# Loading V of three batches densely and spreading it on GpSimd: sparse attention before a squared-ReLU MLP, one core

## The chip, the cores and the metric

The kernel runs on one core of one Trainium2 chip. The metric is the device time of one execution in microseconds; the time given for a kernel is the median of several runs. Below, PE is TensorE, DVE is VectorE, ACT is ScalarE, POOL is GpSimd, and SP is the SyncE, whose queue issues DMAs here.

## The reference

Attention in 8 batches of 8 heads over 576 positions of 64 elements. The first four heads of a batch use a local causal mask (32 wide), the last four a strided one (same position modulo 32). The result becomes a matrix x of 4608 tokens by 512 and goes through an MLP with a squared ReLU.

```python
scores = scale * np.matmul(q, k.transpose(0, 1, 3, 2))
rel = pos[:, None] - pos[None, :]
mask_local = (rel >= 0) & (rel < 32)
mask_strided = (rel >= 0) & (pos[None, :] % 32 == pos[:, None] % 32)
attn = softmax(np.where(mask, scores, -1e9))
x = (attn @ v).transpose(0, 2, 1, 3).reshape(B * S, H * D)
h = np.maximum(x @ w_in, 0.0)
out = (h * h) @ w_out
```

## The kernel before

A unit is one batch and one pair of heads; units 4b and 4b+1 of batch b are local, 4b+2 and 4b+3 strided. A strided unit is gathered so that 8 blocks of 72 rows stand densely, and only those blocks are computed. Each unit has steps: T (transposes of q and k on PE, local units of the early batches), S (scores, matmul at L346 into four PSUM banks, exponentials on ACT at L325, masks on DVE at L360), D (the product with V at L487, in two parts for a local and three for a strided unit, each followed by a reciprocal and a scaling on DVE at L499 and L500, which also free the PSUM bank), and E (the transposition of the result into `xt`). V tiles have a further column of ones, so that a row takes VP = 72 places of which 64 come from memory; the product gives the softmax sum as well.

The MLP runs in 9 chunks of 512 tokens: mm1 (L547, 16 groups of four matmuls, ReLU on ACT at L553, square on DVE at L556) and mm2 (L587, 16 groups). The order is written out by hand: a list of MLP groups, a list of attention steps, and `due`, which says how many attention steps stand ahead of each group. Batches 0 and 1 have an order of their own; batches 2 to 7 are a stream that starts at group 32. `hooks` holds further work to be issued ahead of a given group, put there by `at`, `second` and `plan`. Every engine runs its own instructions in the order in which they were issued, so a waiting instruction holds up what stands behind it on its engine. The MLP and attention share PE in that order.

Loads. DMAs issued from POOL convert f32 to bf16 on the way. For batches 2 to 4 these are:

- `load_qk_local_sw` (L132): rows of q and k of the local units, cast (copied into another layout) later by `cast_qk_local` (L142) on DVE and ACT;
- `cast_str_dram` (L167): q and k of the strided units into a DRAM tile `q_d`, `k_d`, which `transpose_str` (L175) brings in transposed, by a DMA transpose on the SP queue, as `qT_s` and `kT_s`;
- `load_v_local_sw` (L239, L240): V of the local units straight into `vl_all`, in runs of 64 elements;
- `load_v_str_direct` (L689): V of the strided units straight into the tiles `vss` (`vs` in the profile), also in runs of 64 elements, four DMAs per batch.

`load_v_local_gated` puts a one-element copy on POOL ahead of V (L677) that reads the last transposed tile of the batch: so POOL waits for the DMA transposes of that batch, and all that it issues later comes after them. `hold_sync(4)` (L681) is a tiny DMA on SP that reads V of batch 4: so SP's DMA transposes of batch 4 wait for the landing of that V. V and the DMA waits are released through slots: `vls` and `vss` have four tiles each, used by two batches in turn (batches 2 and 4 use the same two).

From batch 5 on, `loads_qk` and `loads_v` load q, k and V as f32 from the SP queue, and POOL casts them (L142, L222, L223, L254). The cast of strided V, `cast_v_str` at L254, is the function that the change uses for batches 2 to 4 as well. `load_v_str_sw(b)` stands in the file before and after; before the change nothing calls it. It loads strided V of one batch in one DMA into a staging tile `v_st` (72 partitions, rows of 512 elements, bf16); a load of the same shape at L439 serves batches 0 and 1.

The vl_st memsets of two staging tiles (L875) stand at hook 50.

Of the kernel before, what the change touches and what calls it, by code (L numbers as in the profile page):

```python
# [9 lines left out]
BF16 = mybir.dt.bfloat16  # L10
# [4 lines left out]
def kernel(  # L15
# [9 lines left out]
    nc = tc.nc  # L25
    B, H, S, D = q.shape
# [7 lines left out]
    NJ = 8  # L34
    RH = STRIDE // NJ
    SP_ = RH * NA
    NBS = 2 * NJ
    VP = 72

    singles = ctx.enter_context(tc.tile_pool(name="singles", bufs=1))  # L40
# [12 lines left out]
    dram = ctx.enter_context(tc.tile_pool(name="dram", bufs=2, space=bass.MemoryType.DRAM))  # L53
# [16 lines left out]
    NV = 4  # L70
# [4 lines left out]
    vl_all = singles.tile([128, NV, 2, NL, VP], BF16, name="vl")  # L75
    vls = [vl_all[:, i] for i in range(NV)]
    vss = [singles.tile([SP_, NBS, VP], BF16, name=f"vs{i}") for i in range(NV)]
    vl_sts = [singles.tile([128, 2 * NL, D], FP32, name=f"vl_st{i}") for i in range(2)]
# [4 lines left out]
    w_in_b = singles.tile([128, 4, d_ff], BF16)  # L83
    w_out_b = singles.tile([128, 16, d_model], BF16)

    ones = singles.tile([128, D], BF16)
    bias_l = w_out_b[:, 12:14, :].rearrange("p a c -> p (a c)")[:, 0:S].rearrange("p (a t c) -> p a t c", a=2, c=QL)
    bias_s = w_out_b[0:SP_, 14, 0:S // 2].rearrange("p (t c) -> p t c", c=SP_)
# [9 lines left out]
    units = [(b, p) for b in range(B) for p in range(H // 2)]  # L98
    st = {}
# [4 lines left out]
    LB = 5  # L104
    PAIRS = 22

    def load_qk_local(u, eng, gate=None):
        b, p = units[u]
        s = st.setdefault(u, {})
        for name, src in (("q", q), ("k", k)):  # L110
            t = qk_st.tile([QL, 2, 6 * D], FP32, name=f"{name}_st")
            if gate is not None and name == "q":
                nc.gpsimd.tensor_copy(t[0:1, 0, 0:1], gate)
            if b >= LB:
                for hh in range(2):
                    eng.dma_start(out=t[:, hh].rearrange("p (t d) -> p t d", d=D),
                                  in_=src[b, 2 * p + hh].rearrange("(t p) d -> p t d", p=QL))
                s[name + "f"] = t
                continue
            eng.dma_start(out=t, in_=src[b, 2 * p:2 * p + 2]  # L120
                          .rearrange("h (p j) d -> p h (j d)", j=6))
            s[name + "f"] = t
# [13 lines left out]
    def cast_qk_local(u, copies, names="qk"):  # L136
        s = st[u]
        for name, copy in zip("qk", copies):
            if name not in names:
                continue  # L140
            t = qk_in.tile([QL, 6, 2, D], BF16, name=f"{name}_l")
            copy(t.rearrange("p j h d -> p h j d"),  # L142
                 s[name + "f"].rearrange("p h (j d) -> p h j d", j=6))
            s[name] = t
# [17 lines left out]
    came = {}  # L162

    def cast_str_dram(b):
        for name, src in (("q", q), ("k", k)):
            t = dram.tile([4 * SP_, NJ * D], BF16, name=f"{name}_d")
            nc.gpsimd.dma_start(  # L167
                out=t.rearrange("(x y) c -> x (y c)", x=16),
                in_=src[b, H // 2:H].rearrange("h (x y) d -> (h x) (y d)", x=4))
            big[b, name] = t  # L170

    def transpose_str(b):
        for name in "qk":
            o = strT.tile([128, NJ // 2, 4 * SP_], BF16, name=f"{name}T_s")
            nc.sync.dma_start_transpose(out=o, in_=big.pop((b, name)))  # L175
            came[b] = o[0:1, 0, 0:1]
            for i in range(2):
                st.setdefault(4 * b + 2 + i, {})[name + "T"] = o[:, :, 2 * SP_ * i:2 * SP_ * (i + 1)]
# [16 lines left out]
    def transpose_local(u):  # L195
        s = st[u]
        for name in "qk":
            if name == "k":
                full = kTl[v_slot(u)]
                dst = full[:, 32:32 + S]  # L200
            else:
                full = dst = qkT.tile([128, S], BF16, name="qk"[u % 2] + "T")
            nc.sync.dma_start_transpose(out=dst.rearrange("c (t p) -> c t p", p=QL),
                                        in_=s[name].rearrange("p t h d -> p (t h d)"))
            s[name + "T"] = full

    def v_slot(u):
        b, p = units[u]
        return (b * 2 + p % 2) % NV
# [18 lines left out]
    def load_v_str_sw(b):  # L228
        t = v_st.tile([SP_, 2, NJ * D], FP32, name="v_st")
        t = t.rearrange("p h c -> p (h c)").bitcast(BF16).rearrange("p (h c) -> p h c", h=4)  # L230
        nc.gpsimd.dma_start(out=t, in_=v[b, 4:8].rearrange("h (p j) d -> p h (j d)", j=NJ))
        for i in range(2):
            st.setdefault(4 * b + 2 + i, {})["vf"] = t[:, 2 * i:2 * i + 2]

    def load_v_local_sw(b, u0=0, nu=2):
        i = (2 * b + u0) % NV
        t = vl_all[:, i:i + nu].rearrange("p u h t d -> p (u h t) d")[:, :, 0:D]
        src = v[b, 2 * u0:2 * (u0 + nu)].rearrange("h (t p) d -> p (h t) d", p=QL)
        nc.gpsimd.dma_start(out=t[32:128], in_=src)  # L239
        nc.gpsimd.dma_start(out=t[0:32, 1:2 * nu * NL], in_=src[64:96, 0:2 * nu * NL - 1])  # L240
        for u in range(nu):
            st.setdefault(4 * b + u0 + u, {})["v"] = vls[i + u]
# [8 lines left out]
    def cast_v_str(u, copy=None):  # L251
        s = st[u]
        t = vss[v_slot(u)]
        (copy or nc.gpsimd.tensor_copy)(t[:, :, 0:D], s["vf"].rearrange("p h (j d) -> p (h j) d", d=D))  # L254
        s["v"] = t
# [417 lines left out]
        load_v_str_first(1)  # L673
        load_w_out(3)

    def load_v_local_gated(b):
        nc.gpsimd.tensor_copy(vl_all[64:65, (2 * b) % NV, 0, 0, 0:1], came[b])  # L677
        load_v_local_sw(b)

    def hold_sync(b):  # L680
        nc.sync.dma_start(out=dram.tile([1, 2], BF16, name="hold"),  # L681
                          in_=vss[v_slot(4 * b + 3)][0:1, NBS - 1, 0:2])

    def load_v_str_direct(b):
        for u in (4 * b + 2, 4 * b + 3):
            t = vss[v_slot(u)]
            h = 2 * units[u][1]
            for i in range(2):
                nc.gpsimd.dma_start(out=t[:, NJ * i:NJ * (i + 1), 0:D],  # L689
                                    in_=v[b, h + i].rearrange("(p j) d -> p j d", j=NJ))  # L690
            st.setdefault(u, {})["v"] = t

    def loads_qk(b):
        for i in range(2):
            load_qk_local(4 * b + i, nc.sync)
        cast_str_dram(b)
        for i in range(2):
            cast_qk_local(4 * b + i, pool2)

    def loads_v(b):  # L700
        for i in range(2):
            load_v_local(4 * b + i, nc.sync)
        for i in range(2):
            load_v_str(4 * b + 2 + i, nc.sync)
        for i in range(2):
            cast_v_local(4 * b + i)
        for i in range(2):
            cast_v_str(4 * b + 2 + i)
# [109 lines left out]
    def at(n, fn):  # L818
        hooks.setdefault(n, []).append(fn)

    def plan(b, g0, g1, n0=None):
        if b < LB:
            at(g0, lambda: transpose_str(b))
            for i in range(2):
                copies = dve2 if b == 2 else (nc.scalar.copy, nc.vector.tensor_copy)
                at(g1 + 2 * i, lambda u=4 * b + i, c=copies: cast_qk_local(u, c))
            return
        g = g0 + (g1 - g0) * 45 // 100
        tr, tl = max(g + 8, g0 + (g1 - g0) * 8 // 10), (g + 14, g + 18)
        at(g, lambda: loads_qk(b))  # L830
        at(tr, lambda: transpose_str(b))
        at(n0, lambda: loads_v(b))
        for i in range(2):
            at(tl[i], lambda u=4 * b + i: transpose_local(u))

    def second(n, *fns):
        for fn in fns:
            at(n, fn)
# [25 lines left out]
    rows = lambda b: (lambda: load_qk_local_sw(b, (4 * b, 4 * b + 1)))  # L864
    second(14, rows(2), lambda: cast_str_dram(2))
    plan(2, 28, 28)
    second(29, lambda: load_v_local_gated(2), lambda: load_v_str_direct(2), rows(3), lambda: cast_str_dram(3))
    done_prev, g_prev = 0, 32
    plan(3, 42, 46)
    second(43, lambda: load_v_local_gated(3), rows(4), lambda: load_v_str_direct(3), lambda: cast_str_dram(4))  # L870
    second(60, lambda: load_v_local_sw(4), lambda: load_v_str_direct(4))
    second(64, lambda: hold_sync(4))
    plan(4, 64, 61)
    for t in vl_sts:
        second(50, lambda t=t: nc.gpsimd.memset(t[0:32], 0.0))  # L875
    for b in range(2, B):
        g_end, s_end = ready.get(b, starts[b]), ends[4 * b + 3]
        total = sum(weights[g_prev:g_end])
# [49 lines left out]
```

## Time and profile before

| | us |
|---|---|
| median of 5 runs (307.31 to 308.35) | 307.95 |
| the profiled execution, whole | 307.48 |
| its span | 305.8 |
| PE busy in the span | 296.6 |
| DVE busy | 158.1 |
| ACT busy | 166.1 |
| POOL busy | 75.4 |

Busy times are shares of the whole span; the stages differ. From 56 to 125 us, where the loads of batches 2 to 5 are issued and used, DVE and ACT are busier than on average: between 66 and 70 us DVE is busy for 3.77 of 4 us and ACT for 3.70, while PE has 3.95. Start times in the timelines below are in us from the start of the span, and the number after the engine's line is the source line. Matmuls overlap in the pipeline, so the time of a group is read from its start to the start of the next one. The chain of waits follows the work that ended last back from the end; a DMA piece in it runs from issue to landing, and other work may have gone on beside it.

### The profile page before, as it was taken

The numbers are of one execution on the slowest core, as the hardware profiler recorded it, in microseconds if no ns is written. First come the engines' busy times: TensorE is split into PE (matmuls) and PEld (weight loads), VectorE is DVE, ScalarE is ACT, GpSimd is POOL, SyncE is SP. The second block draws the span as 40 slices with busy tenths as digits, with TensorE's granted clock in tenths as the row PEclk, the third lists the DMA queues.
The fourth block names the chain that finished last, engine by engine and source line by source line (L and its number), as shares of the span: only waits on it lengthen the run. The fifth ranks groups of instructions, "written<-read, shape, count | busy, mean of one in ns | idle before, by whom it ended". The sixth has DMA issues, their size and how long they took to land.

```text
span 305.8 us, 6066 instructions
## 1 busy us (share of the span) xinstructions
PE 296.6 (97%) x2328; PEld 150.0 (49%) x2368; DVE 158.1 (52%) x406; ACT 166.1 (54%) x335; POOL 75.4 (25%) x105
## 2 busy tenths in 40 slices
PE   8989999999999999999999999999999999999995
PEld 3644464555555544445445545544444444444444
DVE  4558646578777776665748586364422222222200
ACT  4748748787667765545545456453344443444311
POOL 8753300540882033630272060000000000000000
PEclk9999999999999999999999999999999999999999
DMA  8999997996999999999899682122220001000121
GB/s 154 162 204 205 190 208 144 222 167 144 139 200 158 165 201 217 212 191 183 194 253 213 152 194 65 49 71 67 86 68 35 34 35 36 34 34 36 62 76 70
DMA packets 94118, 40.75 MB, mean 133 GB/s; under 512 B 78858, under 2 KB 87754, under 8 KB 93898
## 3 DMA queue, kind: packets, MB, share of 16 engines
q0 software_dynamic: 34528, 15.00, 39.3%
q1 hardware_dynamic: 59562, 25.37, 36.5%
q8 instruction: 18, 0.29, 0.4%
q14 instruction: 10, 0.08, 0.1%
HBM read 37.63 MB, written 13.57 MB: 167 GB/s over the span
## 4 chain that ended last, share of the span: by engine, by line
PE 82%; DMA 6%; issue 6%; POOL 4%; DVE 1%; ACT 0%; POOLq 0%; DVEq 0%
PE ph L547 35%; PE py L587 28%; PE ph L587 4%; PE pt L587 3%; DMA vs<-in_v_dram 3%; PE pt L487 3%; DMA w_out_b<-in_q_dram 2%; PE pt L346 2%; PE pt L547 1%; DMA kT_s<-k_d 1%; PE pt L569 1%; POOL vs L689 1%; PE pt L523 1%; PE pt L410 1%; POOL q_st L132 1%
## 5 line engine op out<-in xcount | busy, mean ns | idle before, releaser
L547 PE MATMUL ph<-xt,w_in_b 128*128 128x512 bf16 x536 | 138.6, 379 | 1.0
L553 ACT ACTIVATE r<-ph 128x512 bf16<-128x512 f32 x138 | 82.3, 597 | 93.9 <-PE ph L547 91.3
L556 DVE TENSOR_TENSOR g_sb<-r 128x512 bf16<-128x512 bf16 x144 | 64.3, 447 | 105.6 <-ACT r L553 104.7
L587 PE MATMUL py<-w_out_b,g_sb 128*128 128x512 bf16 x384 | 100.2, 379 | 0.9 <-issue 0.3
L547 PEld LDWEIGHTS <-w_in_b 128*128 128x128 bf16 x576 | 52.3, 98 | 55.0 <-DMA w_in_b<-in_moe_w_in_dram 0.2
L587 PEld LDWEIGHTS <-g_sb 128*128 128x128 bf16 x560 | 51.4, 98 | 56.2 <-issue 0.2
L325 ACT ACTIVATE e<-pt 128x288 bf16<-128x288 f32 (+1 forms) x86 | 30.5, 408 | 6.9 <-PE pt L346 6.7
L587 PE MATMUL ph<-w_out_b,g_sb 128*128 128x512 bf16 x107 | 27.2, 379 | 0.2
L487 PEld LDWEIGHTS <-e 128*128 128x128 bf16 (+1 forms) x384 | 20.2, 97 | 14.2 <-DVE e L360 0.5
L591 ACT COPY y<-py 128x512 f32<-128x512 f32 x25 | 14.6, 585 | 6.4 <-PE py L587 5.6
L500 DVE TENSOR_TENSOR x_s<-pt,rinv 72x384 bf16<-72x384 f32 (+1 forms) x33 | 16.7, 505 | 1.1
L500 DVE TENSOR_TENSOR x_l<-pt,rinv 96x384 bf16<-96x384 f32 x25 | 13.8, 554 | 0.9
L499 DVE RECIPROCAL rinv<-pt 96x6 f32<-96x6 f32 (+2 forms) x58 | 10.7, 184 | 5.6 <-PE pt L487 5.4
L222 POOL CAST vl<-vl_st 128x768 bf16<-128x768 f32 x6 | 5.7, 944 | 30.8 <-DMA vl_st<-in_v_dram 16.0
L487 PE MATMUL pt<-vs,e 72*128 72x65 bf16 x174 | 11.1, 193 | 0.5 <-DVE x_l L500 0.2
L422 ACT ACTIVATE e<-pt 72x504 bf16<-72x504 f32 (+3 forms) x25 | 10.9, 482 | 0.6 <-PE pt L410 0.6
L587 PE MATMUL pt<-w_out_b,g_sb 128*128 128x512 bf16 x46 | 10.7, 379 | 0.3 <-issue 0.3
L142 POOL CAST q_l<-q_st 96x768 bf16<-96x768 f32 x6 | 5.2, 859 | 19.9 <-ACT r L553 15.5
L689 POOL DMA_DIRECT2D vs<-in_v_dram x12 | 9.7, 817 | 1.0 <-PE pt L346 0.7
L360 DVE TENSOR_TENSOR e<-e,mask_full 128x576 bf16<-128x576 bf16 x20 | 9.0, 450 | 1.9 <-ACT e L325 1.7
L360 DVE TENSOR_TENSOR e<-e,mask_str 72x576 bf16<-72x576 bf16 x16 | 7.7, 486 | 3.8 <-ACT e L325 3.7
L487 PE MATMUL pt<-vl,e 128*128 128x65 bf16 x150 | 8.7, 193 | 0.0
(131 smaller groups left out, 232.3 us busy)
## 6 DMA issues: line engine op xcount, KB each, us to landing
out_dram<-y SPq DMA_DIRECT2D x35, 256.0 KB, 2.8
w_out_b<-in_moe_w_out_dram POOLq DMA_DIRECT2D x4, 512.0 KB, 14.5
q_d<-in_q_dram POOLq DMA_DIRECT2D x6, 288.0 KB, 8.1
k_d<-in_k_dram POOLq DMA_DIRECT2D x6, 288.0 KB, 9.0
q_st<-in_q_dram SPq DMA_DIRECT2D x12, 144.0 KB, 3.5
k_st<-in_k_dram SPq DMA_DIRECT2D x12, 144.0 KB, 5.1
vl_st<-in_v_dram SPq DMA_DIRECT2D x12, 144.0 KB, 3.1
v_st<-in_v_dram SPq DMA_DIRECT2D x6, 288.0 KB
```

The source lines that it names most:

```text
L325: nc.scalar.activation(e[0:kn, lo:lo + S // 2], pss[row][half][0:kn, 0:S // 2], AF.Exp, scale=scale)
L360: nc.vector.tensor_tensor(x, x, m, op=ALU.mult)
L422: nc.scalar.activation(o, x, AF.Exp, scale=scale)
L487: nc.tensor.matmul(po[:, n - n0, :], e[0:kn, pos(n):pos(n) + 128], rhs[0:kn, src(n), 0:D + 1], start=True, stop=True)
L499: nc.vector.reciprocal(rinv[0:w, 0:m], po[0:w, 0:m, D:D + 1])
L500: nc.vector.tensor_tensor(x, po[0:w, 0:m, 0:D], rinv[0:w, 0:m].to_broadcast([w, m, D]), op=ALU.mult)
L547: nc.tensor.matmul(ph, w_in_b[:, kk, 128 * ff:128 * (ff + 1)], xt[kk][:, 512 * c:512 * (c + 1)], start=(kk == order[0]), stop=(kk == order ...
L553: nc.scalar.activation(r, ph, AF.Relu)
L556: later(1, lambda: nc.vector.tensor_tensor(g[:, ff, :], r, r, op=ALU.mult))
L587: nc.tensor.matmul(py, g[:, ff, 128 * j:128 * (j + 1)], w_out_b[:, ff, :], start=(ff == 0), stop=(ff == 15))
L591: nc.scalar.copy(y, py)
L689: nc.gpsimd.dma_start(out=t[:, NJ * i:NJ * (i + 1), 0:D], in_=v[b, h + i].rearrange("(p j) d -> p j d", j=NJ))
```

## The change

Strided V of batches 2 to 4 is now loaded with `load_v_str_sw` into the staging tile and cast into `vss` by POOL (`cast_v_str_pair`). The gate on POOL becomes `hold_pool`, a one-element copy into a tile of its own. V of batch 3 (local and strided) is issued right behind the rows of q and k of batch 3, ahead of `cast_str_dram(3)`, and so also ahead of the DMA transposes of batch 3. The loads of batch 4 stand together at hook 51, behind the gate on the transposes of batch 3: rows, local V, strided V, then `cast_str_dram(4)`; the casts of V follow at hook 60. The hold on SP is gone. A third gate on POOL stands in `loads_qk(5)`, ahead of `cast_str_dram(5)`, and waits for the transposes of batch 4. The memsets of `vl_sts` move from hook 50 to 29, behind the casts of V on POOL. The second of the two casts of local q and k of batches 3 and 4 moves two groups later. In the program that results, the order of PE's instructions is the same as before; on DVE and ACT only the copies `k_l` and `q_l` of units 13 and 17 stand later.

```diff
+    held = singles.tile([1, 1], BF16)
-    def load_v_local_gated(b):
-        nc.gpsimd.tensor_copy(vl_all[64:65, (2 * b) % NV, 0, 0, 0:1], came[b])
-        load_v_local_sw(b)
-
-    def hold_sync(b):
-        nc.sync.dma_start(out=dram.tile([1, 2], BF16, name="hold"),
-                          in_=vss[v_slot(4 * b + 3)][0:1, NBS - 1, 0:2])
-
-    def load_v_str_direct(b):
+    def hold_pool(b):
+        nc.gpsimd.tensor_copy(held, came[b])
+
+    def cast_v_str_pair(b):
         for u in (4 * b + 2, 4 * b + 3):
-            t = vss[v_slot(u)]
-            h = 2 * units[u][1]
-            for i in range(2):
-                nc.gpsimd.dma_start(out=t[:, NJ * i:NJ * (i + 1), 0:D],
-                                    in_=v[b, h + i].rearrange("(p j) d -> p j d", j=NJ))
-            st.setdefault(u, {})["v"] = t
+            cast_v_str(u)
 
     def loads_qk(b):
         for i in range(2):
             load_qk_local(4 * b + i, nc.sync)
+        if b == LB:
+            hold_pool(b - 1)
         cast_str_dram(b)
...
-                at(g1 + 2 * i, lambda u=4 * b + i, c=copies: cast_qk_local(u, c))
+                at(g1 + (4 if b > 2 else 2) * i, lambda u=4 * b + i, c=copies: cast_qk_local(u, c))
...
-    second(29, lambda: load_v_local_gated(2), lambda: load_v_str_direct(2), rows(3), lambda: cast_str_dram(3))
+    second(29, lambda: hold_pool(2), lambda: load_v_local_sw(2), lambda: load_v_str_sw(2), rows(3),
+           lambda: load_v_local_sw(3), lambda: load_v_str_sw(3), lambda: cast_str_dram(3),
+           lambda: cast_v_str_pair(2), lambda: cast_v_str_pair(3))
+    for t in vl_sts:
+        second(29, lambda t=t: nc.gpsimd.memset(t[0:32], 0.0))
     done_prev, g_prev = 0, 32
     plan(3, 42, 46)
-    second(43, lambda: load_v_local_gated(3), rows(4), lambda: load_v_str_direct(3), lambda: cast_str_dram(4))
-    second(60, lambda: load_v_local_sw(4), lambda: load_v_str_direct(4))
-    second(64, lambda: hold_sync(4))
+    second(51, lambda: hold_pool(3), rows(4), lambda: load_v_local_sw(4), lambda: load_v_str_sw(4),
+           lambda: cast_str_dram(4))
+    second(60, lambda: cast_v_str_pair(4))
     plan(4, 64, 61)
-    for t in vl_sts:
-        second(50, lambda t=t: nc.gpsimd.memset(t[0:32], 0.0))
```

The functions called, unchanged by the diff:

```python
    def load_v_str_sw(b):
        t = v_st.tile([SP_, 2, NJ * D], FP32, name="v_st")
        t = t.rearrange("p h c -> p (h c)").bitcast(BF16).rearrange("p (h c) -> p h c", h=4)
        nc.gpsimd.dma_start(out=t, in_=v[b, 4:8].rearrange("h (p j) d -> p h (j d)", j=NJ))
        for i in range(2):
            st.setdefault(4 * b + 2 + i, {})["vf"] = t[:, 2 * i:2 * i + 2]

    def cast_v_str(u, copy=None):
        s = st[u]
        t = vss[v_slot(u)]
        (copy or nc.gpsimd.tensor_copy)(t[:, :, 0:D], s["vf"].rearrange("p h (j d) -> p (h j) d", d=D))
        s["v"] = t
```

## The prediction

> **What bounds the kernel now.** I read the page's engine rows first, then the chain of waits, then the timelines of TensorE (PE), VectorE (DVE) and GpSimd (POOL) where the chain leaves PE.
>
> ```profile
> PE 296.6 (97%) x2328; PEld 150.0 (49%) x2368; DVE 158.1 (52%) x406; ACT 166.1 (54%) x335; POOL 75.4 (25%) x105
> PE 82%; DMA 6%; issue 6%; POOL 4%; DVE 1%; ACT 0%; POOLq 0%; DVEq 0%
> ...
> 80.81 8.72 DMA vs<-in_v_dram
> 89.54 0.04 issue
> 89.58 0.32 PE pt L487 x5
> ```
>
> PE is busy in 97% of the span, and the chain is PE for 82%. The DMA piece before 89.58 looks like 8.7 us of waiting, but beside it PE went on with other work: only the start of one group of matmuls hung on it. The change touches loads and casts used between about 57 and 125 us. So what it can win is the sum of PE's gaps there. PE's timeline shows two:
>
> ```profile
> 72.70 0.49 PE L346 MATMUL pt<-qT_s,kT_s 64*72 64x72 bf16 x16
> 73.39 0.67 PE L487 MATMUL pt<-vs,e 72*128 72x65 bf16 x6 [0.20 <-DVE x_l L500]
> 73.89 1.03 PE L587 MATMUL ph<-w_out_b,g_sb 128*128 128x512 bf16 x4
> 76.14 0.35 PE L487 MATMUL pt<-vs,e 72*128 72x65 bf16 x6
> 76.33 1.03 PE L587 MATMUL ph<-w_out_b,g_sb 128*128 128x512 bf16 x3
> ...
> 88.88 0.47 PE L346 MATMUL pt<-qT_s,kT_s 64*72 64x72 bf16 x16
> 89.28 0.62 PE L487 MATMUL pt<-vs,e 72*128 72x65 bf16 x6
> 89.96 0.81 PE L587 MATMUL ph<-w_out_b,g_sb 128*128 128x512 bf16 x3
> ```
>
> Start to start, six vs matmuls take 76.33-76.14 = 0.19 and sixteen score matmuls 89.28-88.88 = 0.40. At 72.70 it is 0.69 and at 73.39 0.50: 0.29+0.31 = 0.60 lost (first product of unit 10, batch 2). At 89.28 (unit 14, batch 3) it is 0.68 instead of 0.19; one of the next group's four matmuls (0.216 each) is missing from the records, so about 0.28 is lost. Together 0.9 us: no gain can be larger. DVE shows who is late:
>
> ```profile
> 71.93 0.35 DVE L142 COPY k_l<-k_st 96x768 bf16<-96x768 bf16 x1
> 72.20 0.45 DVE L360 TENSOR_TENSOR e<-e,mask_str 72x576 bf16<-72x576 bf16 x1
> ...
> 72.79 0.55 DVE L500 TENSOR_TENSOR x_l<-pt,rinv 96x384 bf16<-96x384 f32 x1
> 73.26 0.45 DVE L360 TENSOR_TENSOR e<-e,mask_str 72x576 bf16<-72x576 bf16 x1
> ...
> 88.83 0.35 DVE L142 COPY k_l<-k_st 96x768 bf16<-96x768 bf16 x1
> 89.10 0.45 DVE L360 TENSOR_TENSOR e<-e,mask_str 72x576 bf16<-72x576 bf16 x1
> ```
>
> The third matmul of each product needs the second row's mask, which ends at 73.26+0.45 = 73.71 and at 89.55. The V that the chain names landed at 80.81+8.72 = 89.53: the mask is as late as V.
>
> **What the Trainium skill says.** Its page "SBUF — State Buffer", section "Who interferes with whom": GpSimd shares one port pair with VectorE, held for a whole instruction; a VectorE operation with two SBUF inputs blocks against a GpSimd one that reads SBUF, a copy in a 2-port mode likewise, one with at most one SBUF input outside those modes does not. The trace agrees:
>
> ```profile
> 110.44 0.82 POOL L142 CAST q_l<-q_st 96x768 bf16<-96x768 f32 x1 [15.47 <-ACT r L553]
> ...
> 110.46 1.08 DVE L556 TENSOR_TENSOR g_sb<-r 128x512 bf16<-128x512 bf16 x1 [0.35 <-ACT r L553]
> ...
> 125.88 2.21 POOL L254 CAST vs<-v_st 72x1024 bf16<-72x1024 f32 x2
> ```
>
> L556 takes 0.43 alone and 1.08 beside a cast (+0.65); the PSUM readers L500 keep 0.55. Its page "DMA: Bandwidth & Descriptors", section "Why small descriptors are slow (HBM only)": each packet has a fixed overhead, large at 256 B. Here it is larger than the 27% stated: by issue plus time to landing in the tile views, the four L689 loads of batch 2 end at 61.47+5.2 = 66.6, the vl loads before them at 63.4, so 3.2 us for 288 KB in rows of 64; the dense q_d and k_d after them (71.0, 72.3) take 1.4 each.
>
> **The change, part by part.**
>
> *V dense.* Per batch four L689 issues (3.24 us on POOL) become one, priced 0.8 by the equal load at L439, and 3.2 us of queue become 1.4. What is added is two POOL casts per batch. L254 shows 1.03 to 1.29 us from f32; a bf16 source is not in the trace. I bound it by half the fastest (0.5, an estimate) and 1.29, and take 1.1.
>
> *V of batch 3 ahead.* POOL's issues after the first hold cost 2.0 (vl), 0.8, 1.4 (rows), 2.0, 0.8, 1.1 (q_d, k_d): done at 57.1+8.1 = 65.2, as before (64.71). The queue then lands v_st of batch 2 at 63.4+1.4 = 64.8, rows at 66.3 and 67.7 (before 68.1, 69.5), vl of batch 3 by 71.9 (3040 rows against 2304 in 3.2 us: 4.2), v_st 73.3, q_d 74.8, k_d 76.2. The SP queue's kT_s transpose, 3.6 us from issue to the hold (72.46 to 76.03), ends at 79.9 instead of 76.0. It is needed at 86.28: six us of cover. Behind it SP has two xt transposes (needed by L547 at 92.17) and y stores (four y buffers): covered. V of batch 2 is cast by 67.2, needed at 73.39: covered. V of batch 3 moves from 89.5 to about 76; but the mask ends at 89.55, so this gains 0 to 0.05, not 0.28.
>
> The casts wait for the landing of v_st; behind them on POOL stand the two memsets of vl_st (1.4 together, moved here) and the second hold. Casts to 75.5 and memsets to 77 end before the hold opens at 79.9: 0.
>
> *Rows of batch 4 wait behind the second hold,* 79.9 instead of 76.0, but no longer behind V. Issued at 80.2 and landing 5.8 later (first of the rows before) they arrive at 86.0 and 87.4, before 85.7 and 87.2. Users: ACT at 88.04, DVE at 88.83. Cover 1.4 us; behind DVE's copy stands the mask of 89.10 and then PE, so beyond that every microsecond counts in full.
>
> *Hold on SP removed, third hold on POOL.* Transposes of batch 4 started at 102.64 after the hold; now q_d and k_d land at about 94 to 96. They are needed at 111.63. The third POOL hold keeps q_d of batch 5 and the q/k casts of batch 5 until about 100; these casts ran from 110.44. All are earlier than before: 0. The 1x1 copies cost 0.35 each on an idle POOL.
>
> *Second q/k cast two groups later.* On DVE k_l (0.35) leaves the run before 73.71, which has no idle time from 70.56 on, and on ACT q_l (0.83) leaves the run of exps into a 1.73 us gap before 76.08. The mask ends at 73.36 and PE gains 0.35 (0.2 if another input is next, 0.6 if all the gap goes). At unit 17 there is no gap: 0.
>
> *What the casts cost.* Casts of batch 2 stand at 64.8 to 67.0; DVE idles 0.95 before 66.10 and 0.63 before 70.56: 0, at most 0.4. Casts of batch 3 stand at 73.3 to 75.5. There DVE would run k_l at 74.5, a mask at 74.8, kTl, a mask at 75.9 and the x_s that frees the fourth PSUM bank of unit 12's scores: at about 77.1, with PE wanting it at 77.15. Cover 0.05. One collision costs 0.65; two at worst 1.1, if the second cast starts just ahead of k_l; none if V lands after 75. I take 0.55. Casts of batch 4, near 93 to 95, meet a bank freed 0.5 before use (95.69 for 96.21): 0 to 0.6, I take 0.1.
>
> Sum: -0.35 + 0.55 + 0.1 - 0.05 = +0.25. Span 305.8 gives 306.05; the profiled run, 307.48, gives 307.7. The median is 307.95, 0.47 above that run: 308.2.
>
> **Rivals.**
>
> *The gain stays, casts hidden.* With casts of 0.5 us, or V landing after 75, only -0.35 to -0.9 remains. For it: DVE idles in both stretches and the late casts from 110 to 183 us moved no PE step visibly. Against: DVE is busy 3.40 of 4 us from 74 to 78, more than there. Worked out: -0.7, 307.25.
>
> *The port lock decides (the slower side).* Place: between 73.0 and 74.4 casts of batch 3 take the port pair ahead of DVE's k_l. Price: 1.1 on DVE, less 0.05 of cover, all on PE's 77.4 scores; it eats the 0.35, and the same lock late at 96.2 adds up to 0.6. Net +0.75 to +1.35; I take +1.0, 308.95. It decides from a lag of about 1.0 us upward. Against: a VectorE request already queued goes between two casts (126.20 between 125.88 and 126.86).
>
> *Transposes too late.* If the longer queue delays the second hold by 3 us more, rows miss their 1.4 us: +1.6, 309.55. Against: six us of other cover, and dense rows drain fast.
>
> **How the numbers follow.** A difference of 0.2% (0.62 us) is about what can be told from no change. Forecast 0.46 (of it 0.05 above 308.57, so slower), hidden casts 0.24 (0.21 faster, 0.03 within), port lock 0.24 (0.22 slower, 0.02 within), late transposes 0.06 (slower). That makes faster 0.21, same 0.46, slower 0.33. The range 307.1 to 309.3 cuts the ends of both sides; the forecast's own is 307.6 to 308.7.
>
> **What would show it.** In the profile after: L254 casts of vs near 65, 73 and 93 us and L360 or L142 on DVE stretched to about 1 us beside them; the product at 73.4 losing 0.25 rather than 0.6; the one at 89.3 still waiting, now for the mask alone; scores of unit 12 near 77.4 waiting for x_s. I am wrong if those scores start on time (faster), if the chain shows q_st or kT_s of batch 4 before a PE piece (slower), or if the gap at 89.3 vanishes with V there.

## The result and the profile after

| | before | after |
|---|---|---|
| median of the runs taken together | 307.76 us (43 runs) | 308.62 us (25 runs) |
| ratio, with its 95% interval | | 1.0035 [1.0024, 1.0046] |
| the profiled execution, whole | 307.48 | 309.20 |
| its span | 305.8 | 307.5 |

The kernel became slower by 0.35%. On 307.76 us that is 1.08 us, with 0.74 to 1.42 as the ends of the interval: more than the 0.2% that can be told from no change. The medians lie only 0.86 us apart, because the runs of the kernel after spread further upward. The forecast was 308.2 us, +0.25 us on its own sum. This ratio and those below leave out runs that took over 1.5% longer than the fastest of the same kernel; here that is one of the 25, at 314.25 us.

From the page of the kernel after, the engine rows, the chain, and two groups (columns: busy time in us, mean ns of one, idle time before them):

```profile
PE 296.8 (97%) x2328; PEld 149.7 (49%) x2368; DVE 160.8 (52%) x406; ACT 166.2 (54%) x335; POOL 74.1 (24%) x103
...
PE 76%; DMA 14%; DVE 5%; issue 2%; ACT 1%; POOL 1%; SPq 0%; DVEq 0%; POOLq 0%
...
L557 DVE TENSOR_TENSOR g_sb<-r 128x512 bf16<-128x512 bf16 x144 | 67.1, 468 | 104.1 <-ACT r L554 103.5
...
L255 POOL COPY vs<-v_st 72x1024 bf16<-72x1024 bf16 x6 | 6.8, 1166 | 17.8 <-DMA v_st<-in_v_dram 17.8
```

PE does the same work in the same time. VectorE is busy 2.7 us longer with the same 406 instructions, and its squares alone take 67.1 us where they took 64.3 (L556, mean 447 ns): that is the mark of being held off, since its durations contain the time for which it was blocked. The six new copies are there with a mean of 1.166 us. Line numbers are those of before plus one. The chain's DMA share of 14% misleads: its pieces of any length (vl, k_st, w_in_b) all end before 51 us, where nothing is changed yet; `kT_s` and the rows of batch 4 are not in it.

To see where the time went I compared the start of each group of matmuls in the two traces; PE's order is the same, so a step in the difference is time lost or won at that place. After stands 1.00 us later at 50.7 us already. Up to some 57 us the two programs are identical, so this is not the change: the other runs below stand between 0.49 us earlier and 0.70 us later than before at the same place. From there on three steps follow: -0.27 at 73.4, +0.58 near 78, and +0.44 between 109.6 and 111.4, in all +0.75. PE's timeline of before has at the second and third place:

```profile
77.41 0.43 PE L346 MATMUL pt<-qT,kTl 64*128 64x96 bf16 x12
...
107.03 2.76 PE L547 MATMUL ph<-xt,w_in_b 128*128 128x512 bf16 x11
109.63 0.35 PE L487 MATMUL pt<-vl,e 128*128 128x65 bf16 x6
```

PE's timeline of after shows the three places and the gap of the second strided unit:

```profile
73.69 0.47 PE L347 MATMUL pt<-qT_s,kT_s 64*72 64x72 bf16 x16
74.12 0.66 PE L488 MATMUL pt<-vs,e 72*128 72x65 bf16 x6
74.62 1.03 PE L588 MATMUL ph<-w_out_b,g_sb 128*128 128x512 bf16 x4
...
78.13 0.34 PE L347 MATMUL pt<-qT,kTl 64*128 64x96 bf16 x7
78.86 0.28 PE L347 MATMUL pt<-qT,kTl 64*128 64x96 bf16 x5 [0.39 <-DVE x_s L501]
...
90.59 0.62 PE L488 MATMUL pt<-vs,e 72*128 72x65 bf16 x6
91.27 0.81 PE L588 MATMUL ph<-w_out_b,g_sb 128*128 128x512 bf16 x3
...
108.34 2.54 PE L548 MATMUL ph<-xt,w_in_b 128*128 128x512 bf16 x10
111.16 0.38 PE L548 MATMUL ph<-xt,w_in_b 128*128 128x512 bf16 x1 [0.28 <-DVE xt L532]
111.38 0.34 PE L488 MATMUL pt<-vl,e 128*128 128x65 bf16 x6
```

From 73.69 to 74.12 are 0.43 where before had 0.69: the gain. The scores of unit 12 stop after seven matmuls and wait for `x_s`: the loss at 78. From 90.59 to 91.27 are 0.68, exactly as before: the gap at unit 14 did not close. At 111.16 the last mm1 matmul waits for a copy of `xt`: from 108.34 to 111.38 are 3.04 us, where before had 2.60. VectorE and GpSimd in the same windows tell who was late:

```profile
75.53 0.35 DVE L143 COPY k_l<-k_st 96x768 bf16<-96x768 bf16 x1
75.79 1.29 DVE L361 TENSOR_TENSOR e<-e,mask_str 72x576 bf16<-72x576 bf16 x1
77.00 0.74 DVE L306 COPY kTl<-pt 128x576 bf16<-128x576 bf16 x1
...
78.25 0.55 DVE L501 TENSOR_TENSOR x_s<-pt,rinv 72x384 bf16<-72x384 f32 x1
...
107.86 1.05 DVE L557 TENSOR_TENSOR g_sb<-r 128x512 bf16<-128x512 bf16 x1 [0.91 <-ACT r L554]
...
109.53 0.91 DVE L557 TENSOR_TENSOR g_sb<-r 128x512 bf16<-128x512 bf16 x1
...
110.37 0.74 DVE L532 COPY xt<-pt 128x576 bf16<-128x576 bf16 x1
```

```profile
66.42 2.21 POOL L255 COPY vs<-v_st 72x1024 bf16<-72x1024 bf16 x2 [1.29 <-DMA v_st<-in_v_dram]
...
74.35 2.42 POOL L255 COPY vs<-v_st 72x1024 bf16<-72x1024 bf16 x2 [5.73 <-DMA v_st<-in_v_dram]
...
98.12 2.21 POOL L255 COPY vs<-v_st 72x1024 bf16<-72x1024 bf16 x2 [10.83 <-DMA v_st<-in_v_dram]
...
107.82 0.82 POOL L143 CAST q_l<-q_st 96x768 bf16<-96x768 f32 x1
...
109.28 0.88 POOL L143 CAST k_l<-k_st 96x768 bf16<-96x768 f32 x1 [0.65 <-DMA k_st<-in_k_dram]
```

The mask of 0.45 us takes 1.29 while the two casts of V of batch 3 run from 74.35 to 76.77; `x_s`, which frees the bank that the scores wait for, comes 0.8 us late. At 107.8 and 109.3 the square L557 takes 1.05 and 0.91 us beside the casts of q and k of batch 5. Those casts are not new; they came at 110.44 before, where they met VectorE's work after the `xt` copy, not ahead of it.

### The profile page after: what moved, and what is told of

Its sections match the earlier page's. It is cut to its first block, busy times and chain, and to the rows that moved or that the text cites. A ratio compares the mean times of both kernels' runs of the same rounds, so it can differ in the third digit from the quotient of the medians.

```text
span 307.5 us, 6052 instructions
## 1 busy us (share of the span) xinstructions
PE 296.8 (97%) x2328; PEld 149.7 (49%) x2368; DVE 160.8 (52%) x406; ACT 166.2 (54%) x335; POOL 74.1 (24%) x103
## 4 chain that ended last, share of the span: by engine, by line
PE 76%; DMA 14%; DVE 5%; issue 2%; ACT 1%; POOL 1%; SPq 0%; DVEq 0%; POOLq 0%
PE ph L548 34%; PE py L588 27%; DMA vl<-in_v_dram 6%; DMA k_st<-in_k_dram 5%; PE ph L588 4%; PE pt L488 3%; DMA w_in_b<-in_moe_w_in_dram 3%; PE pt L588 3%; PE pt L347 1%; DVE e L361 1%; PE pt L570 1%; DVE x_l L501 1%; DVE g_sb L557 1%; PE pt L291 1%; PE pt L411 1%
## 5 line engine op out<-in xcount | busy, mean ns | idle before, releaser
L557 DVE TENSOR_TENSOR g_sb<-r 128x512 bf16<-128x512 bf16 x144 | 67.1, 468 | 104.1 <-ACT r L554 103.5
L255 POOL COPY vs<-v_st 72x1024 bf16<-72x1024 bf16 x6 | 6.8, 1166 | 17.8 <-DMA v_st<-in_v_dram 17.8
L361 DVE TENSOR_TENSOR e<-e,mask_str 72x576 bf16<-72x576 bf16 x16 | 8.5, 539 | 3.8 <-ACT e L326 3.7
L592 ACT COPY y<-ph 128x512 f32<-128x512 f32 x7 | 4.1, 580 | 6.4 <-PE ph L588 6.2
```

What stands on the lines that cost most here:

```text
L361: nc.vector.tensor_tensor(x, x, m, op=ALU.mult)
L557: later(1, lambda: nc.vector.tensor_tensor(g[:, ff, :], r, r, op=ALU.mult))
L592: nc.scalar.copy(y, py)
```

## The experiments

In each of them the time is given as a ratio to runs of the kernel before on the same chip. "A" is the kernel after, "B" the kernel before. Shifts of PE are those of the one profiled execution.

### One strided V less to cast

`e1_no_cast3` (A):

```diff
         for u in (4 * b + 2, 4 * b + 3):
-            cast_v_str(u)
+            if b == 3:
+                st[u]["v"] = vss[v_slot(u - 4)]
+            else:
+                cast_v_str(u)
```

> The changed kernel with the two POOL casts of strided V of batch 3 left out (batch 3 multiplies by the V of batch 2 instead); all loads stay. Port lock: the mask beside the casts falls from 1.29 us back to 0.45, the scores of unit 12 near 78 us lose their 0.39 us wait for x_s, and the kernel is 0.4 to 0.6 us faster than the changed one, about 308.1 against 308.6 (ratio to before about 1.002). Late data (longer queue, later transposes and rows): no difference, 308.6.

1.0501 [1.0459, 1.0543], median 323.75. The edit brought a wait of its own: the tiles that batch 3 now reads are those that the casts of batch 4 write, and the product of unit 14 waited 11.9 us for them. Up to 84 us the trace can be read all the same: no wait at 78, and the gain at 73.4 kept. I repeated it with the tiles of batch 3 filled with zeros early, so that nothing has to wait:

```diff
-            cast_v_str(u)
+            if b == 3:
+                st[u]["v"] = vss[v_slot(u)]
+            else:
+                cast_v_str(u)
...
+    for t in vss[2:]:
+        second(28, lambda t=t: nc.gpsimd.memset(t[:, :, 0:D], 0.0))
```

> The changed kernel with the two POOL casts of strided V of batch 3 left out; the strided heads of batch 3 multiply by a V of zeros that POOL writes beforehand, while it waits. All loads stay. Port lock: the mask near 76 us takes 0.45 instead of 1.29 us, the scores of unit 12 near 78 us start without the 0.39 us wait for x_s, and against the kernel before PE stands 0.5 to 0.6 us better there than with the casts, to the end: ratio to before about 1.0015 instead of 1.0035. Late data: PE stands the same as with the casts.

1.0017 [0.9992, 1.0043], but the median of all its 20 runs is 311.36 us, and ten of them took 311.92 to 319.05. What those ten waited for is not known, so the ratio does not price the casts; what can be read is the trace of one run of 310.68 us. Its VectorE has the mask at its own length, and PE the scores in one piece, but later a wait for rows of batch 4:

```profile
76.01 0.45 DVE L361 TENSOR_TENSOR e<-e,mask_str 72x576 bf16<-72x576 bf16 x1
```

```profile
78.35 0.43 PE L347 MATMUL pt<-qT,kTl 64*128 64x96 bf16 x12
...
90.23 0.24 PE L488 MATMUL pt<-vs,e 72*128 72x65 bf16 x2
91.24 0.30 PE L488 MATMUL pt<-vs,e 72*128 72x65 bf16 x4 [0.78 <-DVE e L361]
```

So the wait at 78 goes with the casts of batch 3. In this run the rows of batch 4 landed at 90.44 and cost 0.69 us at unit 14, and scores of unit 20 waited 1.52 us for `kTl`: places where A was on time, by little at the first.

### The same casts at another time

`e2_cast3_late` (A), casts of batch 3 behind the rows of batch 4:

```diff
-           lambda: cast_v_str_pair(2), lambda: cast_v_str_pair(3))
+           lambda: cast_v_str_pair(2))
...
-    second(51, lambda: hold_pool(3), rows(4), lambda: load_v_local_sw(4), lambda: load_v_str_sw(4),
+    second(51, lambda: hold_pool(3), rows(4), lambda: cast_v_str_pair(3), lambda: load_v_local_sw(4), lambda: load_v_str_sw(4),
```

> The changed kernel with the two casts of batch 3 moved on POOL behind the second hold and the rows of batch 4, so near 84 to 86 us instead of 74.4 to 76.8. Port lock at that place: the wait at 78 us goes, as without the casts, -0.5 us, unless the masks near 85 us are hit the same way (then 0). Late data: local V, strided V and q_d/k_d of batch 4 go 2.2 us later, so no gain or slower.

1.0014 [0.9989, 1.0038]. No wait at 78; the collision has only moved. VectorE and GpSimd of this run:

```profile
83.85 1.88 DVE L361 TENSOR_TENSOR e<-e,mask_full 128x576 bf16<-128x576 bf16 x1 [0.34 <-ACT e L326]
```

```profile
83.38 2.04 POOL L255 COPY vs<-v_st 72x1024 bf16<-72x1024 bf16 x2
```

The mask waits from 83.85 until both casts are through at 85.42, and PE loses 0.66 us at 87.5. The first cast ends at 84.44, so the second went ahead of a VectorE instruction that was already waiting: the price of a pair of casts can be their sum, not one of them. This run does not show the loss at 109.6, although its casts of q and k of batch 5 ran at 107.77 and 109.17, within 0.11 us of A's: its VectorE was half a microsecond ahead of A's there.

### The hold on SP

`e5_after_sp_hold` (A with a tiny DMA on SP behind the transposes of batch 4, so that SP's loads of batch 5 come later), and `e6_before_no_hold` (B without the hold):

```diff
             at(g0, lambda: transpose_str(b))
+            if b == 4:
+                at(g0, lambda: nc.sync.dma_start(out=dram.tile([1, 2], BF16, name="hold"),
+                                                 in_=st[18]["kT"][0:1, 0, 0:2]))
```

```diff
     second(60, lambda: load_v_local_sw(4), lambda: load_v_str_direct(4))
-    second(64, lambda: hold_sync(4))
```

> The changed kernel with a tiny DMA on SP behind the transposes of batch 4 that reads their result, so that the loads of q and k of batch 5 wait for it, near 106.3 us as in the kernel before (106.65) instead of 102.7. Port lock: the q/k casts of batch 5 go back from 107.8 to about 110.4 us, out of the stage of mm1 alone, and the 0.44 us that PE lost up to 111.2 go: about 308.2. Late data: nothing gained, since the loads come later.

> The kernel before with only the hold on SP taken out. Transposes of batch 4 start at about 94 to 96 us instead of 102.6, the loads of q and k of batch 5 and their POOL casts follow some 5 to 8 us earlier (from about 103), in the stage of mm1 alone. Port lock there: PE loses 0.2 to 0.5 us between 100 and 111 us (ratio 1.001). If earlier loads are harmless: ratio 1.000. If the transposes collide with V of batch 4 in the DMA queues: V of batch 4 lands later than 102.2, still ahead of its use, ratio 1.000.

e5: 1.0023 [1.0002, 1.0044]. The casts of batch 5 begin at 111.83 instead of 107.82, the squares keep 0.43 and 0.42 us, and the loss at 109.6 is gone. That fits a loss by these casts and does not prove it: e1b, e2, e7 and e9 run without this hold, as A does, begin these casts between 104.70 and 112.24, and have no loss there either. For the casts speak the two stretched squares beside them in A's trace. The loss at 78 stays (+0.58). Later the scores of unit 20 wait for `kTl`, +0.31: the loads that were too early for VectorE are now too late for PE. e6: 1.0025 [1.0006, 1.0045]. Not in this ratio are six of its 20 runs, which took 312.83 to 321.53 us; of 63 runs of before on the same chip none was above 309.87. No trace shows such a run. The expectation that loads of batch 5 would come earlier failed; they came later. SP's queue and PE of e6:

```profile
94.83 5.79 SPq L175 DMA_TRANSPOSE kT_s<-k_d  x1
100.71 1.52 SPq L116 DMA_DIRECT2D q_st<-in_q_dram  x2
102.32 5.80 SPq L116 DMA_DIRECT2D k_st<-in_k_dram  x2
```

```profile
126.84 0.34 PE L346 MATMUL pt<-qT,kTl 64*128 64x96 bf16 x7 [0.55 <-DMA kTl<-k_l]
```

Without the hold the transposes start while V of batch 4 is still landing in runs of 64 elements, and issuing them takes 5.79 us where B, after the hold, took 1.30. All of SP's loads behind them slip, up to the scores at 126.84 that before had no wait.

### The shift of the second cast

`e3_before_shift` is B with the q/k casts of the second unit two groups later, `e7_after_no_shift` is A without that:

```diff
-                at(g1 + 2 * i, lambda u=4 * b + i, c=copies: cast_qk_local(u, c))
+                at(g1 + (4 if b > 2 else 2) * i, lambda u=4 * b + i, c=copies: cast_qk_local(u, c))
```

> The kernel before with only the second q/k cast of batches 3 and 4 two groups later. By the forecast's step the mask of unit 10 ends 0.35 us earlier and PE gains 0.25 to 0.35 us at 73.4 that it keeps: about 307.45 against 307.76. Rival: k_l only moves within a full stretch of DVE, x_s comes at the same time as before and the scores of unit 12 near 77.4 give it back: 307.76.

> The changed kernel with the second q/k cast of batches 3 and 4 back in its old place. Forecast's step: the mask of unit 10 ends 0.35 us later and the product at 73.4 loses 0.6 again instead of 0.3, but k_l is then out of the way of the POOL casts, so x_s near 78 us comes up to 0.35 us earlier: together 0 to +0.1 us against the changed kernel. If the shift is worth its 0.25 us by itself: +0.25.

e3: 1.0003 [0.9982, 1.0024]; PE gains 0.27 at 73.4 and keeps it up to 83.8. Then it is lost: the transposes of batch 3 took longer (hold open at 77.89), V of batch 3 behind them was late, and PE waited for it:

```profile
84.57 0.31 PE L487 MATMUL pt<-vl,e 128*128 128x65 bf16 x5 [0.58 <-DMA vl<-in_v_dram]
...
90.37 0.19 PE L487 MATMUL pt<-vs,e 72*128 72x65 bf16 x1 [0.33 <-DMA vs<-in_v_dram]
```

In B's own profile that V landed at 83.76 for a use at 83.83. So B has an exposure there that its profile did not show as a wait, and which V of batch 3 ahead of the transposes removes. e7: 1.0039 [1.0012, 1.0067]. No gain at 73.4, as expected. But against VectorE's work the casts came 0.9 us later: the first starts 0.52 ahead of the mask (74.47, 74.99) where in A it was 1.44 (74.35, 75.79). This time the mask got in between the two casts and took 0.83, a second one 0.62, and PE lost only 0.03 at 78. In its place the rows of batch 4 were late by 0.55 us and the gap at unit 14 grew by 0.64.

### Parts put together without the casts

`e8_direct_rows_early` (B with the shift, V of batch 3 as before in runs of 64 but ahead of `q_d` and `k_d`, rows of batch 4 ahead of the gate; the hold on SP stays):

```diff
-    second(29, lambda: load_v_local_gated(2), lambda: load_v_str_direct(2), rows(3), lambda: cast_str_dram(3))
+    second(29, lambda: load_v_local_gated(2), lambda: load_v_str_direct(2), rows(3), lambda: load_v_local_sw(3), lambda: load_v_str_direct(3),
+           lambda: cast_str_dram(3), rows(4))
...
-    second(43, lambda: load_v_local_gated(3), rows(4), lambda: load_v_str_direct(3), lambda: cast_str_dram(4))
+    second(43, lambda: hold_pool(3), lambda: cast_str_dram(4))
```

> A version from what was learned: the kernel before with the second q/k cast two groups later, V of batch 3 loaded straight into its tiles ahead of q_d and k_d of batch 3 (no POOL casts of V), the rows of batch 4 behind k_d of batch 3 and ahead of the second hold, the hold on SP kept. If the port lock and V behind the hold are what costs: PE gains 0.27 at 73.4 and keeps it, no PE wait at 78 or 111, and V of batch 3 is there early whatever the transposes take: ratio 0.998 to 0.9995. If the longer queue makes the transposes of batch 3 late (needed near 86.3): a wait for kT_s there and 1 us or more lost, ratio above 1.002.

0.9981 [0.9966, 0.9995], median 307.44: a little faster than B, and faster than A. Its profiled run took 308.29 us, the second longest of the 20. It shows no gain at 73.4, because `k_l` had to wait for rows of batch 3 (they landed at 71.15; in before at 69.52), and a loss of 0.24 at unit 14:

```profile
71.17 0.36 DVE L143 COPY k_l<-k_st 96x768 bf16<-96x768 bf16 x1 [0.88 <-DMA k_st<-in_k_dram]
```

So where its 0.19% comes from was not settled; that V of batch 3 no longer comes late as in e3 is likely, not shown. From this version I made two steps back towards A, one at a time. `e10_cast3_alone` loads V of batch 3 dense and casts it, nothing else; `e11_direct_no_hold` takes only the hold on SP away:

```diff
-    second(29, lambda: load_v_local_gated(2), lambda: load_v_str_direct(2), rows(3), lambda: load_v_local_sw(3), lambda: load_v_str_direct(3),
-           lambda: cast_str_dram(3), rows(4))
+    second(29, lambda: load_v_local_gated(2), lambda: load_v_str_direct(2), rows(3), lambda: load_v_local_sw(3), lambda: load_v_str_sw(3),
+           lambda: cast_str_dram(3), rows(4),
+           lambda: cast_v_str(14), lambda: cast_v_str(15))
```

```diff
-    second(64, lambda: hold_sync(4))
```

> The version with direct V and early rows (0.9981 of before), with one thing changed: V of batch 3 strided is loaded dense and cast twice by GpSimd. Theory (the casts hold DVE off near 74 to 77 us and x_s of unit 11 frees the bank late): a mask of about 1.3 us or more on DVE beside the casts, PE loses 0.4 to 0.6 us near 78, ratio to before 0.9995 to 1.0005, so about 0.2% more than without the casts. Rival (casts hidden, other parts of the change cost the time): no PE shift near 78, ratio 0.998.

> The version with direct V and early rows, without the hold on SP ahead of the transposes of batch 4. Theory (without the hold the transposes fall among the loads of V of batch 4, and SP's loads for batch 5 come later): transposes issued near 93 to 95 us take 5 us or more, casts of q and k of batch 5 come at 111 us or later, scores of unit 20 near 126.5 wait 0.3 to 0.7 us for kTl, ratio to before 0.999 to 1.001. Rival (the hold costs nothing when it goes, as the prediction had it): ratio 0.998, no wait at 126.

e10: 1.0014 [0.9999, 1.0030], above e8 by 0.33% (combining the two half-widths, 0.12 to 0.54%; 0.4 to 1.7 us). VectorE and PE of e10 show A's picture again, to a hundredth:

```profile
75.24 1.29 DVE L361 TENSOR_TENSOR e<-e,mask_str 72x576 bf16<-72x576 bf16 x1
```

```profile
77.59 0.34 PE L347 MATMUL pt<-qT,kTl 64*128 64x96 bf16 x7
78.31 0.28 PE L347 MATMUL pt<-qT,kTl 64*128 64x96 bf16 x5 [0.38 <-DVE x_s L501]
...
185.18 0.41 PE L411 MATMUL pt<-kT,kTl 64*128 64x96 bf16 x11 [0.37 <-DVE x_s L501]
```

Against e8, PE loses 0.57 between 73.6 and 78.5, and another 0.57 by 185. There the casts of local V of a later batch, which all kernels here have, ran from 179.22 and held a square (1.05 us) and a mask (1.07 us); in e8 they began at 181.48, and both had their own length: whether such a cast costs something depends on when it falls. The difference of the two ratios is therefore not the price of the casts of batch 3. In these two traces e10 also wins 0.26 at 73.4 and 0.24 at unit 14 against e8, so that up to 170 us only 0.08 is lost in sum. What the casts of batch 3 cost is read at 78 alone.

e11: 1.0206 [1.0167, 1.0244]. SP's queue and PE:

```profile
92.22 2.15 SPq L176 DMA_TRANSPOSE qT_s<-q_d  x1
94.47 14.03 SPq L176 DMA_TRANSPOSE kT_s<-k_d  x1
108.55 2.68 SPq L117 DMA_DIRECT2D q_st<-in_q_dram  x2
```

```profile
119.02 0.70 PE L347 MATMUL pt<-qT_s,kT_s 64*72 64x72 bf16 x16 [8.08 <-DMA kT_s<-k_d]
```

The same collision as in e6, shown here by the longest of six runs (317.06 us; the shortest took 311.98): the four strided V loads of batch 4 landed at 99.2 to 116.1 instead of 101.2 to 102.6, the second transpose took 14.03 us to issue, and PE stood for 8 us. The expectation had the mechanism, but its size (0.999 to 1.001) was far too small, and PE waited at an earlier place.

### Rows of batch 4 early, in the kernel after

`e9_after_rows_early`:

```diff
-           lambda: load_v_local_sw(3), lambda: load_v_str_sw(3), lambda: cast_str_dram(3),
+           lambda: load_v_local_sw(3), lambda: load_v_str_sw(3), lambda: cast_str_dram(3), rows(4),
...
-    second(51, lambda: hold_pool(3), rows(4), lambda: load_v_local_sw(4), lambda: load_v_str_sw(4),
+    second(51, lambda: hold_pool(3), lambda: load_v_local_sw(4), lambda: load_v_str_sw(4),
```

> The changed kernel with the rows of batch 4 issued behind k_d of batch 3 instead of behind the second POOL hold. Theory (port lock at 78 us and the loads of batch 5 cost most, the rows of batch 4 only in some runs): rows land near 81 us, k_l of unit 17 near 90 never waits for a DMA, PE keeps +0.5 to +0.6 us at 78 and some +0.3 to +0.5 later; ratio to before 1.001 to 1.003. Rival (the rows of batch 4 are the main loss): ratio 1.000 or below.

1.0062 [1.0043, 1.0081]: worse than A. The rows landed at 77.17 and 78.64, so nothing near 90 waits for them, but GpSimd issues the rows ahead of the casts of batch 2, which now run at 68.12 instead of 66.42. VectorE, GpSimd and PE of e9:

```profile
67.83 2.63 DVE L361 TENSOR_TENSOR e<-e,mask_full 128x576 bf16<-128x576 bf16 x1
...
73.30 1.29 DVE L361 TENSOR_TENSOR e<-e,mask_str 72x576 bf16<-72x576 bf16 x1
```

```profile
68.12 2.02 POOL L255 COPY vs<-v_st 72x1024 bf16<-72x1024 bf16 x2
73.03 2.45 POOL L255 COPY vs<-v_st 72x1024 bf16<-72x1024 bf16 x2 [2.89 <-DMA v_st<-in_v_dram]
```

```profile
70.52 0.33 PE L488 MATMUL pt<-vl,e 128*128 128x65 bf16 x5 [1.06 <-DVE e L361]
71.22 0.20 PE L488 MATMUL pt<-vl,e 128*128 128x65 bf16 x1 [0.38 <-DVE e L361]
...
75.33 0.24 PE L488 MATMUL pt<-vs,e 72*128 72x65 bf16 x2 [0.74 <-DVE x_l L501]
```

Casts of batch 2, which cost PE nothing in A's trace, cost 1.8 us here, moved by 1.7 us; at those of batch 3 PE stands another 0.7 later than before. The first mask takes 2.63 us in place of 0.45: it ends at 70.46, 0.3 after the second cast. It began 0.29 us ahead of the first, while GpSimd still issued a DMA; what held it during that time the trace does not say. The later one, at 73.30, ends at 74.59 and so waited for one cast only. So whether rows of batch 4 matter was not told by this run; that a small delay on GpSimd's queue decides the price of the casts was.

## Why the prediction was right and where it was off

**Right.** *The bound and the largest gain.* PE stayed at 97%, and no edit won more than 0.6 us (e8). *The shift:* forecast -0.35 (bounds 0.2 to 0.6), measured -0.27 in A and -0.27 alone on B (e3); in e8 late rows took it away. *V of batch 3 early gains next to nothing at unit 14:* the interval 0.68 there is the same with V landed at 74.3; the mask alone keeps it. *Casts of batch 3:* cast 1.03 to 1.44 us against 1.1 taken, with PE losing 0.58 against 0.55, through the very mask and `x_s` named. The loss stands in A, in e5 and in e10, which adds these casts alone to e8; it is gone in e1, e1b and e2, where they are left out or moved. The rival of hidden casts fell with the bf16 copy being as slow as one from f32. The rival with the port lock at unit 13's `k_l` did not happen as written: `k_l` stayed at 0.35, and the mask behind it was hit. The Trainium skill, "SBUF — State Buffer", section "Who interferes with whom", has the lock held for the whole instruction and the other engine fully blocked; the traces here agree that it blocks (1.29 us beside one cast for a mask of 0.45).

**Off: one collision at 0.65 as the usual price.** The prediction argued that a VectorE request already queued goes between two casts. It did in e7 and at 73.30 of e9, but not in e2 and at 67.83 of e9, where the second cast began when the mask had long been waiting: 1.88 and 2.63 us beside pairs of 2.04 and 2.02. With the mask's own 0.45 taken off, the delays were 0.84 in A, 1.43 and 2.18; 0.65 for one and 1.1 for two were too low. Of A's 0.84 PE lost 0.58, so the size at 78 agreed only because the cover was larger too, some 0.26 instead of 0.05.

**Off: "casts of batch 2: 0, at most 0.4", and late casts that "moved no PE step visibly".** In A's trace the casts of batch 2 cost PE nothing, but that trace is the exception. In e1, e1b, e2, e5 and e7, which have the same casts, the first square beside them took 0.87 to 1.29 us and PE lost 0.18 to 0.58 us by 70. VectorE of A, then of e5, which is the same program up to 100 us:

```profile
67.10 0.63 DVE L557 TENSOR_TENSOR g_sb<-r 128x512 bf16<-128x512 bf16 x1 [0.95 <-ACT r L554]
```

```profile
66.64 0.87 DVE L557 TENSOR_TENSOR g_sb<-r 128x512 bf16<-128x512 bf16 x1 [0.95 <-ACT r L554]
```

In e9, moved by 1.7 us, they cost 1.8, and late casts cost 0.57 in e10. The casts start when a DMA lands, so their place varies from run to run. The forecast priced them at one place.

**Off: "All are earlier than before: 0".** For the q and k casts of batch 5 this is the step that failed in A's trace. Earlier meant onto another part of VectorE's row, ahead of a copy of `xt` that PE needs: +0.44, where the forecast put 0. Five other kernels without the SP hold or with another one (e1b, e2, e5, e7, e9) lose nothing there, so this is what the forecast left open, not what the change always costs. I had asked whether they would be late, not what they would hit. PE shows no step at the casts of batch 4 (98.12), priced 0.1, nor at the third hold.

**Right for a reason that was not given: the removal of the SP hold.** On kernels with V in runs of 64 the hold is worth 0.25% (e6, without its six long runs) or 2.25% (e11 against e8). In A's trace nothing collides, because its V stands ahead of `q_d` and `k_d` on GpSimd's queue: V landed at 98.0, `q_d` at 99.02, and the transposes began at 99.07, so there was no V left to collide with. The forecast had the transposes at 94 to 96 and did not ask what the hold kept apart. That A loses nothing at all by the removal is not shown: the intervals of A and e5 overlap.

**Off: the rows of batch 4.** Forecast to land at 86.0 and 87.4 with 1.4 us of cover; they landed at 88.41 and 89.88. Dense V of batch 2 took 2.9 us after local V instead of 1.4, and `kT_s` 4.5 us from issue to hold instead of 3.6, two mis-sized terms of the same sum. The 1.4 had been set against 3.2 us for the same V in rows of 64, both read from landings. In e8 the loads of batch 3 in such rows landed 1.41 us after local V, so these gaps do not measure the layout, and no run here shows what the dense layout by itself gains. In A's profile the copy still came in time; in e1b and e7 it waited 0.60 and 0.55 us and PE lost 0.69 and 0.64 at unit 14. The rival "transposes too late" had this place.

**The sum.** Forecast: -0.35 + 0.55 + 0.1 - 0.05 = +0.25. A's profile: -0.27 + 0.58 + 0.44 = +0.75. Measured: +1.08 (0.74 to 1.42), or +0.86 between the medians. By size this lies in what the port-lock rival named (+0.75 to +1.35), though the wait is not at the instruction that it named. That 308.62 us is still inside the forecast's own 307.6 to 308.7 is in part luck: the forecast started from 307.95 us, where the runs above gave 307.76. The +0.75 of one profile is not a budget either: its +0.44 stands in no other trace, and its 0 for the casts of batch 2 is the exception. The exposures of the last paragraphs, rows of batch 4, casts of batch 2 and `kTl` of batch 5, each appear in some traces with 0.2 to 1.8 us and in others not at all; how often they strike A was not measured. That they strike now and then fits the spread: A's runs reach from 307.56 to 314.25 us, those of before beside them from 306.62 to 308.89 (on the chip of e1, e2, e3 and e5 one of 59 reached 313.62), and e8's from 306.73 to 308.38.

## What to carry to other kernels

A GpSimd copy put beside a loaded VectorE is priced by the moment at which it starts, and when a DMA starts it that moment moves from run to run: price a pair of back-to-back copies at up to their sum on whatever VectorE instruction they may meet, not at the one that the timeline of before shows there. When work becomes ready earlier, ask whose row it now falls on, as well as whether it is late. Before a hold is taken away, find out which two streams it keeps apart; in this kernel it was transposes and loads of V, and the collision cost up to 8 us of PE.

## What was not expected

Issuing the transpose of `kT_s` on SP took 1.30 us behind the hold (before and e8), and 5.79 (e6) and 14.03 us (e11) while loads in runs of 64 elements were in flight; the last of these landed 13.5 us later than with the hold (116.1 against 102.6, e11 and e8). The Trainium skill, "DMA: Bandwidth & Descriptors", section "Issuing engines are not separate DMA queues", says that all DMAs share the same 16 engines and interleave; the runs agree, and the size of the loss is what they add. Whether dense loads in flight would hold the transposes up as much was not tested: A has its V not only dense but also ahead of them.

Start-up, which no edit touches, put PE at 50.7 us between 0.49 us earlier and 1.00 us later than in the profile of before. A difference of two single profiles below 1 us therefore says nothing by itself; steps at one place do. Even a step counts only when it returns: the one at 78 stands in three traces, the one at 109.6 in one.
